# Attention and token/channel mixer on one core: token weights as fp32 over SyncE's queue, first half of c1 in three pieces, more dummies, two opening runs in another order

## The chip, the cores and the metric

One core of one Trainium2 chip runs the kernel. The metric is the time on the device in microseconds (us), the median of three runs: 340.75 us for the kernel before (340.21 to 340.96).

## What is computed

```python
def _attn_ref(q, k, v):                    # 8 batches, 12 heads, 448 tokens, 64 per head
    scores = scale * np.matmul(q, k.transpose(0, 1, 3, 2)) - np.log(S)
    attn = 1.0 / (1.0 + np.exp(-scores))
    return np.matmul(attn, v)

def _moe_ref(x, w_tok1, w_tok2, w_ch1, w_ch2):   # x: 8 x 448 x 768, the heads side by side
    h = np.maximum(x.transpose(0, 2, 1) @ w_tok1, 0.0) @ w_tok2     # 448 -> 256 -> 448
    u = x + h.transpose(0, 2, 1)
    h2 = np.maximum(u @ w_ch1, 0.0) @ w_ch2                         # 768 -> 1536 -> 768
    return u + h2
```

All inputs and the output are fp32; the kernel computes in fp16 with fp32 sums.

## The kernel before

A batch has three units of four heads (two pairs: `g` 0 and 1 on the partitions, `hi` 0 and 1 beside each other), so there are 24 units; the 448 tokens are seven rows `j` of 64. A unit's path is: `q` and `k` are transposed (`tr_q`, `tr_k`), seven score steps `qk(b, u, j)` (L180 to L201: four matmuls of 64x64 into a bank pair of which there are two, then one sigmoid on ScalarE, L194), the value product `av` (L218) into `xa`, copied by VectorE to `xu` (L227), a transpose of `xu` to `xn` (on TensorE with a copy by VectorE in `xtrans`, L252 and L257, or by a transposing DMA from SyncE, L243), the first token product `tok1` (L296, weights `w1`, result in `tk`) with a ReLU to `h`, and the second, `ytrans` (L316, weights `w2`), added to `xu` (L326). When a batch's three units are done, channel products follow: `ch1` (weights `c1`, L364) and `ch2` (weights `c2`, L584). From the second batch on these use seven products in place of eight (`sevens`, L514; L814, L861).

Every engine works its instructions off in the order in which the code lists them (`manual_schedule`); what differs is only how long one waits for another. All loads go through GpSimd's queue (POOL, kind software_dynamic), which also casts fp32 to fp16 under way, and are listed at L945 to L1002: the first `k`, then `q`, `k`, `v` of batch 0 by unit, `w1` (three DMAs, L961 and L965), `w2s` (one, L967), the rest of `v`, batch 1's `q` and `k`, the first half of `c1` (all six 128-row blocks, L976), and so on to `c2` and batch 2. SyncE's queue (SP, kind hardware_dynamic) loads one half of `first_q` at the start; after that its next instruction is the transposing DMA of the second batch's second unit, at 56.30 us, then come the transposes of `q`, `k` and the stores.

The opening (batch 0, L1065 to L1123) is written out by hand: 16 dummy matmuls (`keep_warm`, L1028, on a tile of zeros) stand before the first transposes; then three units of seven scores with other work between them (`between`). `w1` has 448 rows = seven rows `j` of 64, kept as `w1[128, 4, 256]`: rows 2t and 2t+1 in the lower and upper partitions of block t, and row 6 in the lower half of block 3. Its upper half is zeroed at L951 for the first four units and filled with row 6 again by a later DMA (L1189), since `tok_tail` (L277) reads it from both halves. `w2s` is regrouped to `w2` by VectorE (L1051).

The first channel product of batch 0 (`ch1(0, 0, 0, 4)` and two more) takes its blocks in the order 0, 3, 1, 4, 2, 5 (`BY_UNIT`): unit 0's two blocks, unit 1's, unit 2's.

Then two runs written in one loop (L1146 to L1201, `c` 4 and 5: second and third unit of batch 1) weave seven scores, the value product of the unit before and a pair of columns of `ch1` (`ch1_pair`, L387: matmuls of 64x64 in two "turns" of six steps; in the second turn the row halves change places, so each bank gets the other half of the sum). From batch 3 on, `steady(b, u)` (L1305) runs the same plan for each batch; `copies` holds the eight pieces that relayout the next batch's `k` and `q` (L129) and start their transposing DMAs, and `within`, `behind` (L1308) say how many of them are issued at two places of each unit. `gated_loads` (L1125) issues the loads of a later batch after a small copy on GpSimd that waits for the transposed `q`.

Of the kernel before, what the change touches and what calls it, by code (L numbers as in the profile page):

```python
# [9 lines left out]
FP16 = mybir.dt.float16  # L10
# [11 lines left out]
NJ = 7  # L22
NP = 64
NU = 3
# [6 lines left out]
def kernel(  # L31
# [39 lines left out]
    turned = pc.tile([128, 1], FP32, name="turned")  # L71
    w2s = pa.tile([128, 2, S], FP16, tag="parts", bufs=4, name="w2s")
    first_q = pa.tile([128, 2, NJ, E], FP32, tag="parts", bufs=4, name="first_q")
# [14 lines left out]
    def bank(shape, dtype, name):  # L88

        if opening_banks:  # L90
            n = opening_banks.pop(0)
        else:
            n = at_bank[0]
            at_bank[0] = (n + 1) % 4
        return pp.tile(shape, dtype, tag=f"m{n}", bufs=1, name=name)
# [300 lines left out]
    def ch1_pair(b, cb):  # L396

        ps = [bank([128, 512], FP32, f"c1_{b}_{cb + p}") for p in range(2)]

        def step(turn, n):  # L400
            quads(
                ps,
                S,
                turn,
                lambda p, part, m: c1[
                    part, BY_UNIT[n], 128 * (cb + p) + m : 128 * (cb + p) + m + 64
                ],
                lambda p, part: ut(b, BY_UNIT[n])[part, 0:S],
                n == 0,
                n == NDB - 1,  # L410
            )

        def end():
            for p in range(2):
                ch1_out(b, cb + p, ps[p])

        turns = [[lambda t=t, n=n: step(t, n) for n in range(NDB)] for t in range(2)]
        return turns[0], turns[1], end
# [530 lines left out]
    for b in range(2):  # L949
        nc.vector.memset(xu(b)[:, :, :, S:512], 0.0)  # L950
    nc.vector.memset(w1[64:128, 3, :], 0.0)  # L951
    load_first_k(2, NJ)
# [4 lines left out]
    load(0, "k", k, 2, NU)  # L957
    tok_rows = moe_w_tok1.rearrange("(p j) t -> j p t", j=NJ)
    for par in range(2):
        part = slice(64 * par, 64 * par + 64)  # L960
        nc.gpsimd.dma_start(  # L961
            out=w1[part, 0:3, :],
            in_=tok_rows[0:6].rearrange("(t par) p c -> par p t c", par=2)[par],
        )
    nc.gpsimd.dma_start(out=w1[0:64, 3, :], in_=tok_rows[NJ - 1])  # L965
    load(0, "v", v, 1, 2)
    nc.gpsimd.dma_start(  # L967
        out=w2s[:, :, :], in_=moe_w_tok2.rearrange("(tc t) s -> t tc s", tc=2)
    )
    load(0, "v", v, 2, NU)  # L970
    load(1, "q", q, 0, 1)
    load(1, "k", k, 0, 1)

    def load_c1(half):
        cols = slice(CC // 2 * half, CC // 2 * half + CC // 2)
        nc.gpsimd.dma_start(  # L976
            out=c1[:, :, cols],
            in_=moe_w_ch1.rearrange("(db d) c -> d db c", db=NDB)[:, :, cols],
        )

    def load_c2(half):
# [4 lines left out]
        )  # L986

    load(1, "q", q, 1, 2)
    load(1, "k", k, 1, 2)
    load_c1(0)  # L990
    load(1, "v", v, 0, 1)
# [4 lines left out]
    load(2, "q", q, 0, 1)  # L996
    load(2, "k", k, 0, 1)
    load_c2(0)
    load(2, "k", k, 1, NU)
    load(2, "q", q, 1, NU)  # L1000
    load_c2(1)
# [36 lines left out]
    heat[0] = bank([128, 512], FP32, "heat")  # L1038
    keep_warm(16)

# [6 lines left out]
    pe_transpose(0, "k", 0, 0, 2)  # L1047
    keep_warm(3)

    def regroup_w2():  # L1050
# [10 lines left out]
    def tok(u):  # L1061
# [7 lines left out]
            [lambda: keep_warm(4)],  # L1069
            [tp(0, 1, "q")],  # L1070
            [lambda: keep_warm(4)],
# [5 lines left out]
            [value(0, 3, NJ)],  # L1077
            [tp(0, 2, "q")],
            [tp(0, 2, "k")],
# [66 lines left out]
    for c, cb in ((N_FIRST, 3), (N_FIRST + 1, 8)):  # L1146
# [11 lines left out]
        turn0, turn1, end = ch1_pair(0, cb)  # L1158
        if c > N_FIRST:
            qk(b, u, 0)  # L1160
        qk(b, u, 1)
        for f in turn0:
            f()
        qk(b, u, 2)
        av(*before, 0, 4)
        qk(b, u, 3)
        av(*before, 4, NJ)
        if c - 1 in ON_DMA:
            xtrans_dma(*before)
        qk(b, u, 4)  # L1170
        for f in turn1[:4]:
            f()
        qk(b, u, 5)
        for f in turn1[4:]:
            f()
        end()
        qk(b, u, 6)
        if u == 2:
# [7 lines left out]
        if c == N_FIRST:  # L1186
            tok1(*before)
            whole(cb + 4)
            nc.gpsimd.dma_start(out=w1[64:128, 3, :], in_=tok_rows[NJ - 1])  # L1189
            ytrans(*before)  # L1190
        else:
            for w, f in pieces_ch2(0, by_half[:2]):
                f()
                if copies:
                    copies.pop(0)()
            while copies:
                copies.pop(0)()

            nc.gpsimd.tensor_copy(out=gate[:, :], in_=tr[2, "q"][:, 1, NJ - 1, 126:128])
            load(2, "v", v, 1, NU)  # L1200
            gated_loads(b)  # L1201
# [103 lines left out]
    def steady(b, u):  # L1305

        lot, before, ahead = b - 2, divmod(NU * b + u - 1, NU), divmod(NU * b + u - 2, NU)
        within, behind = ((0, 1), (3, 4), (0, 0))[u]  # L1308

# [43 lines left out]
        else:  # L1353
# [5 lines left out]
            run(steps, 5)  # L1359
            send = end(put_off=True)  # L1360
            score()
            at_bank[0] = Y
# [26 lines left out]
        some(behind)  # L1389
        if u == 1 and b < B - 1:  # L1390
            gated_loads(b)
# [102 lines left out]
```

## Time and profile before

| what | value |
|---|---|
| median of three runs | 340.75 us (340.21 to 340.96) |
| profiled execution: time, span from first to last instruction | 341.39 us, 339.6 us |
| first score's sigmoid starts | 8.33 us |
| first matmul on `c1` | 33.70 us |
| two runs of the loop: from, to | 39.3 us, 59 us |
| first `steady` batch: from, to; the next | 102.5 to 140.8 us; 140.8 to 179.1 us |
| first-half `c1` load: issue, landing after | 21.01 us, 12.6 us |
| TensorE's granted clock over the span | 0.998 |

The profiled execution's span is 1.8 us shorter than its time, and its time 0.64 us above the median; times within a trace are counted from the first instruction. In the views of the profile, PE is TensorE's matmuls, PEld its weight loads, DVE VectorE, ACT ScalarE, POOL GpSimd, SP SyncE. A row of the timeline has its start, its length, engine, line, operation, what it writes and reads, how many instructions it merges, and in brackets how long the engine was idle before it and what released it.

### The profile page before, as it was taken

The numbers are of one execution on the slowest core, as the hardware profiler recorded it, in microseconds if no ns is written. First come the engines' busy times: TensorE is split into PE (matmuls) and PEld (weight loads), VectorE is DVE, ScalarE is ACT, GpSimd is POOL, SyncE is SP. The second block draws the span as 40 slices with busy tenths as digits, with TensorE's granted clock in tenths as the row PEclk, the third lists the DMA queues.
The fourth block names the chain that finished last, engine by engine and source line by source line (L and its number), as shares of the span: only waits on it lengthen the run. The fifth ranks groups of instructions, "written<-read, shape, count | busy, mean of one in ns | idle before, by whom it ended". The sixth has DMA issues, their size and how long they took to land.

```text
span 339.6 us, 10285 instructions
## 1 busy us (share of the span) xinstructions
PE 332.2 (98%) x4423; PEld 242.5 (71%) x4423; DVE 234.9 (69%) x484; ACT 213.0 (63%) x272; POOL 58.7 (17%) x102
## 2 busy tenths in 40 slices
PE   7999999999999999999999999999999999999994
PEld 4555565555796679866896679866896679769852
DVE  2277366678998973877768773878758654876882
ACT  3997657388647895578647895578647795314200
POOL 8981550050031000220032002020010000000000
PEclk9999999999999999999999999999999999999999
DMA  7999999999999999998999899988995293028007
GB/s 119 173 174 195 206 205 204 163 175 237 169 187 189 140 168 211 185 142 161 204 145 172 138 206 175 206 117 134 196 175 93 56 193 73 2 56 185 4 11 197
DMA packets 104381, 52.17 MB, mean 154 GB/s; under 512 B 76432, under 2 KB 101264, under 8 KB 104336
## 3 DMA queue, kind: packets, MB, share of 16 engines
q1 hardware_dynamic: 78704, 29.11, 47.8%
q0 software_dynamic: 25168, 21.50, 42.1%
q10 hardware_dynamic: 464, 0.92, 1.0%
q8 instruction: 34, 0.56, 0.7%
q14 instruction: 11, 0.09, 0.1%
HBM read 43.45 MB, written 11.01 MB: 160 GB/s over the span
## 4 chain that ended last, share of the span: by engine, by line
PE 86%; DMA 5%; POOL 4%; ACT 2%; issue 1%; DVE 0%; ACTq 0%; POOLq 0%
PE c_ab L514 14%; PE c L814 10%; PE qk L187 9%; PE c_c L514 8%; PE xa L218 7%; PE c L861 6%; PE tk L296 5%; PE yt L316 5%; PE c L387 4%; DMA c<-in_moe_w_ch_dram 4%; PE c L584 4%; PE c L364 3%; PE c L669 3%; PE c L650 2%; ACT att L194 2%; DMA raw_v<-in_v_dram 2%
## 5 line engine op out<-in xcount | busy, mean ns | idle before, releaser
L194 ACT ACTIVATE att<-qk,att_bias 128x896 f16<-128x896 f32 x168 | 156.0, 1012 | 38.6 <-PE qk L187 37.6
L187 PE MATMUL qk<-tr_q,tr_k 64*64 64x448 f16 x672 | 61.3, 360 | 0.3 <-ACT att L194 0.2
L514 PEld LDWEIGHTS <-c 128*128 128x128 f16 x504 | 48.4, 98 | 1.1 <-issue 0.3
L218 PE MATMUL xa<-att,raw_v 64*64 64x448 f16 x644 | 40.7, 349 | 0.0
L187 PEld LDWEIGHTS <-tr_k 64*64 64x64 f16 x672 | 25.2, 105 | 19.0 <-issue 11.9
L514 PEld LDWEIGHTS <-sum 128*128 128x128 f16 x378 | 36.3, 98 | 0.0
L227 DVE CAST xu<-xa 128x448 f16<-128x448 f32 x40 | 23.1, 619 | 18.8 <-PE xa L218 18.4
L535 ACT ACTIVATE pt_ab<-c_ab 128x896 f32<-128x896 f32 x21 | 19.2, 917 | 20.6 <-PE c_ab L514 20.6
L218 PEld LDWEIGHTS <-raw_v 64*64 64x64 f16 x672 | 22.0, 107 | 8.3 <-issue 0.4
L861 PE MATMUL c<-c,h 64*64 64x384 f16 x360 | 24.6, 322 | 0.0
L1127 POOL COPY gate<-tr_q 128x2 f16<-128x2 f16 x6 | 1.6, 275 | 121.7 <-DMA tr_q<-rel_q 121.7
L326 DVE TENSOR_TENSOR xu<-xu,yt 128x448 f16<-128x448 f16 x38 | 21.7, 613 | 0.0
L537 ACT ACTIVATE h<-c_ab 128x896 f16<-128x896 f32 x7 | 6.4, 917 | 24.4 <-PE c_ab L514 24.4
L296 PE MATMUL tk<-xn,w 128*128 128x256 f16 x156 | 21.2, 274 | 0.1
L544 DVE TENSOR_TENSOR h<-pt_ab,c_ab 128x896 f16<-128x896 f32 x14 | 15.2, 1084 | 8.6 <-PE c_ab L514 8.6
L544 DVE TENSOR_TENSOR h<-pt_c,c_c 128x448 f16<-128x448 f32 x21 | 12.9, 614 | 11.7 <-PE c_c L514 11.6
L316 PE MATMUL yt<-w,h 128*128 128x448 f16 x88 | 20.3, 353 | 0.0
L841 DVE TENSOR_TENSOR o<-un,c 128x384 f32<-128x384 f16 x32 | 17.4, 550 | 4.0 <-PE c L814 4.0
L310 ACT ACTIVATE h<-tk 128x256 f16<-128x256 f32 x42 | 14.2, 406 | 9.5 <-PE tk L296 9.5
L814 PEld LDWEIGHTS <-hid 128*128 128x128 f16 x132 | 12.9, 98 | 8.0
L514 PE MATMUL c_ab<-diffs,c 128*128 128x224 f16 x168 | 18.4, 259 | 0.0
L296 PEld LDWEIGHTS <-w 128*128 128x128 f16 x156 | 13.6, 98 | 5.7 <-issue 2.4
(134 smaller groups left out, 572.1 us busy)
## 6 DMA issues: line engine op xcount, KB each, us to landing
out_dram<-o SPq DMA_DIRECT2D x41, 192.0 KB, 3.2
c<-in_moe_w_ch_dram POOLq DMA_DIRECT2D x4, 1152.0 KB, 16.1
raw_k<-in_k_dram POOLq DMA_DIRECT2D x10, 336.0 KB, 6.9
raw_q<-in_q_dram POOLq DMA_DIRECT2D x10, 336.0 KB, 5.7
raw_v<-in_v_dram POOLq DMA_DIRECT2D x10, 336.0 KB, 8.8
out_dram<-o SPq DMA_DIRECT2D x15, 96.0 KB, 2.4
raw_q<-in_q_dram POOLq DMA_DIRECT2D x12, 112.0 KB, 5.1
raw_k<-in_k_dram POOLq DMA_DIRECT2D x12, 112.0 KB, 5.4
```

Source lines behind the costliest of these rows:

```text
L187: nc.tensor.matmul(out=ps[64 * g : 64 * g + 64, hi, 0:S], lhsT=tr[b, "k"][64 * hi : 64 * hi + 64, u, j, 64 * g : 64 * g + 64], rhs=tr[b, " ...
L194: nc.scalar.activation(out=att[b, u, j][:, :, :], in_=ps[:, :, 0:S], func=SIGMOID, bias=bias_t[:, :], scale=att_scale,)
L218: nc.tensor.matmul(out=ps[g][64 * hi : 64 * hi + 64, 0:S], lhsT=raw[b, "v"][64 * g : 64 * g + 64, u, hi, j, :], rhs=att[b, u, j][64 * g : ...
L227: nc.vector.tensor_copy(out=xu(b)[:, u, g, 0:S], in_=ps[g][:, 0:S])
L296: nc.tensor.matmul(out=ps[tcb], lhsT=w1[rows, t, cols], rhs=xn[b, u][rows, :, t, :], start=(t == 0 and not with_scores), stop=(t == (2 if ...
L316: nc.tensor.matmul(out=ps[:, 0:S], lhsT=h1[b, u][:, tcb, g, :], rhs=w2[:, tcb, :, :], start=(tcb == 0), stop=(tcb == 1),)
L326: nc.vector.tensor_tensor(out=x, in0=x, in1=ps[:, 0:S], op=ADD)
L514: nc.tensor.matmul(out=ps[:, g, p, :], lhsT=weights[n][:, d, 128 * cb : 128 * cb + 128], rhs=moving[n][:, d, :], start=(n in (1, 5, 2) and ...
L535: nc.scalar.activation(out=shaped(part[:, :, :]), in_=ps, func=COPYF)
L544: nc.vector.tensor_tensor(out=shaped(dst), in0=shaped(parts[gs, which]), in1=ps, op=ADD)
L814: nc.tensor.matmul(out=ps[:, 0:DH], lhsT=self.weights[n][:, k, :], rhs=self.moving[n][:, k, :], start=(n in (1, 2, 5) and k == 0), stop=(k ...
L861: nc.tensor.matmul(out=ps[m : m + 64, 0:DH], lhsT=lhsT(n)[part, m : m + 64], rhs=rhs(n)[part, :], start=(opens and turn == 0 and n == 0), ...
```

## The change

- `w1` and `w2s` are loaded as fp32 (`w1s`, `w2s`) by five DMAs on SyncE's queue. They stand behind a memset of one column of `w1s` on VectorE that is listed after the copy of unit 1's `tr_q`. VectorE casts `w1s` to `w1` in one instruction (`cast_w1`), listed between the copies of unit 2's `tr_q` and `tr_k`; both halves of block 3 get row 6, so the zeroing of L951 and the DMA of L1189 go. `regroup_w2` reads fp32.
- The GpSimd queue: without the token weights; `v` of units 1 and 2 in one pair of DMAs; the first half of `c1` by unit (blocks 0 and 3; 1 and 4; 2 and 5), the first piece ahead of batch 1's second unit; batch 2's `k` and `q` of unit 1 ahead of the first half of `c2`.
- 21 dummies in place of 16 at the start.
- In the two runs each score stands one place earlier: `qk` 2 comes after three of the six steps of the first turn, the others follow, and no score is left between the second turn and the plain columns; the third unit's `qk` 0 moves into the first run. `ch1_pair` gets `turn_over`, a copy of one column by VectorE between the turns.
- In batch 3, during which the fifth batch (4) is given its relayouts, the eight pieces are dealt (0, 0), (4, 2), (2, 0) in place of (0, 1), (3, 4), (0, 0), and `gated_loads(3)` comes at the end of unit 2, not 1.

```diff
-    w2s = pa.tile([128, 2, S], FP16, tag="parts", bufs=4, name="w2s")
+    w2s = pa.tile([128, 2, S], FP32, tag="parts", bufs=4, name="w2s")
+    w1s = pa.tile([128, 4, TT], FP32, tag="un", bufs=2, name="w1s")
...
     def ch1_pair(b, cb):
...
+        turn_bank[0] = ps[1]
...
-    nc.vector.memset(w1[64:128, 3, :], 0.0)
...
-    for par in range(2):
-        part = slice(64 * par, 64 * par + 64)
-        nc.gpsimd.dma_start(
-            out=w1[part, 0:3, :],
-            in_=tok_rows[0:6].rearrange("(t par) p c -> par p t c", par=2)[par],
-        )
-    nc.gpsimd.dma_start(out=w1[0:64, 3, :], in_=tok_rows[NJ - 1])
-    load(0, "v", v, 1, 2)
-    nc.gpsimd.dma_start(
-        out=w2s[:, :, :], in_=moe_w_tok2.rearrange("(tc t) s -> t tc s", tc=2)
-    )
-    load(0, "v", v, 2, NU)
+    load(0, "v", v, 1, NU)
...
+    load_c1(0, 0)
     load(1, "q", q, 1, 2)
     load(1, "k", k, 1, 2)
-    load_c1(0)
+    load_c1(0, 1)
+    load_c1(0, 2)
...
+    load(2, "k", k, 1, 2)
+    load(2, "q", q, 1, 2)
     load_c2(0)
-    load(2, "k", k, 1, NU)
-    load(2, "q", q, 1, NU)
+    load(2, "k", k, 2, NU)
+    load(2, "q", q, 2, NU)
...
-    keep_warm(16)
+    keep_warm(21)
...
+    def load_token_weights():
+        rows = moe_w_tok1.rearrange("(p j) t -> j p t", j=NJ)
+        nc.vector.memset(w1s[:, 0, 0:1], 0.0)
+        for par in range(2):
+            part = slice(64 * par, 64 * par + 64)
+            nc.sync.dma_start(
+                out=w1s[part, 0:3, :],
+                in_=rows[0:6].rearrange("(t par) p c -> par p t c", par=2)[par],
+            )
+            nc.sync.dma_start(out=w1s[part, 3, :], in_=rows[NJ - 1])
+        nc.sync.dma_start(
+            out=w2s[:, :, :], in_=moe_w_tok2.rearrange("(tc t) s -> t tc s", tc=2)
+        )
+
+    def cast_w1():
+        nc.vector.tensor_copy(out=w1[:, :, :], in_=w1s[:, :, :])
...
-            [tp(0, 1, "q")],
+            [tp(0, 1, "q"), load_token_weights],
...
-            [tp(0, 2, "q")],
+            [tp(0, 2, "q"), cast_w1],
...
-        if c > N_FIRST:
-            qk(b, u, 0)
         qk(b, u, 1)
-        for f in turn0:
+        for f in turn0[:3]:
             f()
         qk(b, u, 2)
+        for f in turn0[3:]:
+            f()
+        turn_over(turn_bank[0])
+        qk(b, u, 3)
         av(*before, 0, 4)
-        qk(b, u, 3)
+        qk(b, u, 4)
         av(*before, 4, NJ)
...
-        qk(b, u, 4)
+        qk(b, u, 5)
         for f in turn1[:4]:
             f()
-        qk(b, u, 5)
+        qk(b, u, 6)
         for f in turn1[4:]:
             f()
         end()
-        qk(b, u, 6)
...
             tok1(*before)
+            qk(*ahead, 0)
             whole(cb + 4)
-            nc.gpsimd.dma_start(out=w1[64:128, 3, :], in_=tok_rows[NJ - 1])
...
-        within, behind = ((0, 1), (3, 4), (0, 0))[u]
+        within, behind = (
+            ((0, 0), (4, 2), (2, 0)) if b == NU else ((0, 1), (3, 4), (0, 0))
+        )[u]
...
             send = end(put_off=True)
+            some(within)
             score()
...
-        if u == 1 and b < B - 1:
+        if u == (2 if b == NU else 1) and b < B - 1:
             gated_loads(b)
```

More of the change, by code (lines that the diff above doesn't have):

```diff
@@ L410, in step @@
                 n == NDB - 1,
+                True,
             )
@@ L957, with load_c1 @@
     load(0, "k", k, 2, NU)
-    tok_rows = moe_w_tok1.rearrange("(p j) t -> j p t", j=NJ)
-    for par in range(2):
-        part = slice(64 * par, 64 * par + 64)
-        nc.gpsimd.dma_start(
-            out=w1[part, 0:3, :],
-            in_=tok_rows[0:6].rearrange("(t par) p c -> par p t c", par=2)[par],
-        )
-    nc.gpsimd.dma_start(out=w1[0:64, 3, :], in_=tok_rows[NJ - 1])
-    load(0, "v", v, 1, 2)
-    nc.gpsimd.dma_start(
-        out=w2s[:, :, :], in_=moe_w_tok2.rearrange("(tc t) s -> t tc s", tc=2)
-    )
-    load(0, "v", v, 2, NU)
+    load(0, "v", v, 1, NU)
     load(1, "q", q, 0, 1)
     load(1, "k", k, 0, 1)
-    def load_c1(half):
+    def load_c1(half, u=None):
         cols = slice(CC // 2 * half, CC // 2 * half + CC // 2)
+        blocks = slice(0, NDB) if u is None else slice(u, NDB, NU)
         nc.gpsimd.dma_start(
-            out=c1[:, :, cols],
-            in_=moe_w_ch1.rearrange("(db d) c -> d db c", db=NDB)[:, :, cols],
+            out=c1[:, blocks, cols],
+            in_=moe_w_ch1.rearrange("(db d) c -> d db c", db=NDB)[:, blocks, cols],
         )
```

## The prediction

> **What bounds the kernel now.** I read the page first, then the timeline of the opening, that of the two runs, and last what single DMA issues took.
>
> ```profile
> PE 332.2 (98%) x4423; PEld 242.5 (71%) x4423; DVE 234.9 (69%) x484; ACT 213.0 (63%) x272; POOL 58.7 (17%) x102
> ...
> DMA  7999999999999999998999899988995293028007
> ```
>
> TensorE is busy nearly throughout, and the DMA engines (third part of the slices) are full from the second slice to the eighteenth. The two full `steady` batches take 38.3 us each by the stages, with TensorE busy all of it, so little is to be had after 100 us; the change works ahead of that. The opening's timeline:
>
> ```profile
> 1.05 3.59 PE L1028 MATMUL heat<-warm 128*128 128x256 f16 x16 [1.05 <-DVE att_bias L948]
> ...
> 5.83 0.96 PE L170 MATMUL tp_q<-ident,raw_q 128*64 128x128 f16 x14 [1.18 <-DVE raw_q L1041]
> ...
> 7.68 0.96 PE L187 MATMUL qk<-tr_q,tr_k 64*64 64x448 f16 x8
> ...
> 8.33 1.91 ACT L194 ACTIVATE att<-qk,att_bias 128x896 f16<-128x896 f32 x2 [1.01 <-PE qk L187]
> ...
> 10.01 0.55 PE L187 MATMUL qk<-tr_q,tr_k 64*64 64x448 f16 x4
> ...
> 10.61 11.94 ACT L194 ACTIVATE att<-qk,att_bias 128x896 f16<-128x896 f32 x13 [0.38 <-PE qk L187]
> ...
> 11.34 0.58 PE L170 MATMUL tp_q<-ident,raw_q 128*64 128x128 f16 x14
> ...
> 11.96 0.62 DVE L179 COPY tr_q<-tp_q 128x896 f16<-128x896 f16 x1 [2.11 <-PE tp_q L170]
> ...
> 18.04 0.61 DVE L179 COPY tr_k<-tp_k 128x896 f16<-128x896 f16 x1
> ...
> 18.93 0.69 DVE L257 COPY xn<-xb 128x1024 f16<-128x1024 f16 x1 [0.28 <-PE xb L252]
> ...
> 20.07 1.05 PE L296 MATMUL tk<-xn,w 128*128 128x256 f16 x8
> ```
>
> ScalarE sets the pace: from 10.61 its sigmoids follow each other without a gap. TensorE starts slow: 14 transposes take 0.96 us at 5.83 and 0.58 at 11.34, four scores 0.55 at 10.01 and 0.38 later. Ahead of 5.83 TensorE is idle for 1.18 us.
>
> ```profile
> 33.70 0.49 PEld L364 LDWEIGHTS <-c 128*128 128x128 f16 x4 [0.41 <-DMA c<-in_moe_w_ch_dram]
> ...
> 44.42 0.38 PE L187 MATMUL qk<-tr_q,tr_k 64*64 64x448 f16 x4 [0.16 <-ACT att L194]
> 44.43 0.11 PEld L187 LDWEIGHTS <-tr_k 64*64 64x64 f16 x3 [0.58 <-issue]
> ...
> 56.49 0.11 PEld L187 LDWEIGHTS <-tr_k 64*64 64x64 f16 x3 [0.37 <-issue]
> ```
>
> Here TensorE waits: once for `c1`, and in each run for ScalarE before the seventh score (a bank pair is still being read). The last view is the landing time of four issues on SyncE's queue, taken in windows that begin at 56.0, 98.1, 98.7 and 133.5 us:
>
> ```profile
> xn<-xu SPq DMA_TRANSPOSE x1, 10.1
> ```
> ```profile
> out_dram<-o SPq DMA_DIRECT2D x1, 96.0 KB, 5.2
> ```
> ```profile
> out_dram<-o SPq DMA_DIRECT2D x1, 96.0 KB, 6.6
> ```
> ```profile
> out_dram<-o SPq DMA_DIRECT2D x1, 96.0 KB, 2.3
> ```
>
> The same store lands in 2.3 us with GpSimd's queue empty and in 5.2 and 6.6 us with 336 KB loads of that queue under way; a transposing DMA took 10.1 us while `c2` was loading.
>
> **The start.** Sixteen dummies take 3.59 us, so 21 take 3.59 x 21/16 = 4.7 and end at 5.76, just ahead of the transposes at 5.83: nothing is delayed. What it buys is the fast pace sooner. TensorE came to it between 9.65 (last slow dummies) and 10.48, some 4.2 us after 5.83; 4.2 us after 1.05 would be 5.3. Then the 14 transposes save 0.38, the four of `k` 0.43 - 0.58 x 4/14 = 0.26, the three dummies 0.82 - 0.50 = 0.32: 0.96 at most for the first sigmoid, nothing if the pace comes after 7.7. To this comes that the 0.38 gap of ScalarE before its third sigmoid closes, as the work in it (ten transposes, three dummies) shrinks as well. That is 1.34 if the pace comes by 5.8 and 0.4 if it comes after 7.7. VectorE's and ScalarE's copies on this path (0.43, 0.49) do not shrink, so I take 1.0. The Trainium skill (TensorE: Matmul & The Clock Gate, section Part 1: The HAM clock gate) has the clock judged over free-running windows of about 3.4 us, of which one must be busy. By that the pace would come anywhere from 4.5 to 7.9 us; at the late end 0.4 of the start would be left and the sum below would be -0.8 in place of -1.4. That the trace's pace came near 10 us, between one and two such windows after 5.83, agrees with it.
>
> **The token weights.** GpSimd loses five issues of 0.5 to 0.74 us, and SyncE gets five in a stretch where nobody is queued behind them until 56.30. They wait for a memset behind `tr_q`'s copy, which ended at 12.59 and would end at 11.6. At 0.65 us an issue (rows of 0.5 to 0.77 on that queue) the fourth, the last of `w1`, is issued at 13.55. Its landing is the open term. Bounds: 2.3 us (empty queue) and 10.1. The loads of GpSimd's queue ahead of it here are 112 and 224 KB, not 336: the 2.9 us that the first store lost scales to 1.9. So 13.55 + 2.3 + 1.9 = 17.8. VectorE is ready for the cast at 18.04 - 1.0 = 17.1 and is held for 0.7. Behind the cast stand `tr_k`'s copy (unit 2's scores wait for it) and `xn` (the first token product waits). The cast is priced by the `xn` row, 1024 elements in 0.69 (at most twice the 0.43 of the 512-element cast at 5.35, 0.86). Then 17.8 + 0.1 + 0.69 + 0.61 + 0.69 less two overlaps of 0.08 = 19.75, where TensorE would be ready at 19.07. ScalarE has no slack there, as its gap before the next sigmoid is 0.04, so all of it counts: against 20.07 the opening gains 0.3 of the 1.0. Each microsecond of landing is a microsecond of the result.
>
> `regroup_w2` reads fp32 in place of fp16: 0.88 now; between 0.88 and twice that. It is followed by a product that waits for it (0.35 in the trace); I take +0.05, as rows per element of fp32 casts are no slower than copies, +0.9 at the far end. Its load is issued 0.65 later than `w1`'s last and needed 3 us later, which covers it. The memset and `turn_over` (0.15 each, rows of L852) fall into idle time of VectorE (1.88 us before the value copy at 42.62); without that cover each costs 0.15.
>
> **c1 in pieces.** The last weight load before it ends at 33.29 (0.41 ahead), and others follow within 0.1, so 0.3 is lost to `c1`. Of its 1152 KB, 5.7 us at the 206 GB/s of that stage, the first two thirds now suffice to go on, which is 1.9 us sooner, and the token weights have left the queue. Batch 1's second `q` and `k` move behind the first piece: they landed at 23.7 and 25.9 and are read at 31.5. Gain 0.3, range 0 to 0.4. Two more issues of 0.84 on GpSimd are covered, as it sits idle for 6.74 us at 27 to 34.
>
> **The two runs.** Place by place, with four scores 0.19 us of TensorE, 24 quarter matmuls 1.17, sixteen of the value product 0.75 and twelve 0.56: the first run's plain columns start 5.41 us after its first score (39.33 to 44.74), by the sum without a wait 4.9. In the new order the scores are 0.75 to 0.94 apart, at or above the 0.89 of a sigmoid, so the wait goes: 0.5. The second run loses 0.11 and 0.29 to the same: 0.4. I take 0.85; if the waits only move, 0.
>
> **Batch 2 and the fifth batch.** `k` and `q` of unit 1 come ahead of `c2`'s half, which landed at 53.56, is read at 60.09 and comes some 2 us later: covered, by 4 us. In batch 3 the pieces move on VectorE, 0.53 each, but SyncE's transposes of `k` and `q` are issued at 117.5 and 128.85, behind a store and the 5 us transposing issue of `un`; `q`'s last relayout would end near 122. `gated_loads` waits for the same landing (134.59). Nothing moves: 0, -0.1 to +0.5 (the stage is TensorE's).
>
> **Sum.** -0.3 (opening) + 0.05 - 0.3 - 0.85 = -1.4 against the span of 339.6, or 341.39 - 1.4 = 340.0 for the profiled execution. That execution is 0.64 above the median, so from 340.75: 339.3.
>
> **Rivals.** (1) The token weights land in time, by 17.0. Then the start's whole 1.0 is kept: -1.0 - 0.3 - 0.85 = -2.15: 338.6. For it: the loads are small, and the queue is not deep at 12 us (loads land 4.7 us after issue, of which 2 to 3 are their own). Against it: four of them in a row. The Trainium skill (DMA: Bandwidth & Descriptors, section Queues, rings and completion order) says that an engine takes turns between queues after 9 to 17 descriptors. By that rule the loads would have a turn every microsecond, which is this rival; the 10.1 us of the transpose disagree.
>
> (2) Slower: SyncE's loads are served only after the backlog of GpSimd's queue, as the transpose at 56.30 was. Place: the cast on VectorE. It turns the sum positive when the fourth load takes over 5.6 us (17.8 + 1.4 = 19.2). At the 6.6 of the second store, landing at 20.15, it is +1.0: 341.7; at 10.1 it is +4.4: 345.2. For it: two of the three loaded rows are above 5.6. Against it: these had 336 KB or `c2` loads ahead.
>
> (3) The gains don't add: the runs' waits only move to the next place, or the earlier work meets DMAs that don't come earlier (the transpose of 56.30 lands at 66.36 and is read at 68.4; the next at 74.76, read at 76.34, 1.6 us of room). Then -0.3 - 0.3 = -0.6 and 340.1, no change that can be told.
>
> **Chances.** Forecast 0.42, (1) 0.28, (2) 0.13, (3) 0.17. The forecast's own range is 338.8 to 340.0. The range of 8 in 10 runs from 338.2 (rival 1 with 1.3 at the start) to 341.6 (rival 2 at its mildest). A change of 0.2% (0.7 us, 340.07 and 341.43) is about what can be told from none here: faster takes the forecast but for 0.02, (1), and a quarter of (3), 0.72; slower (2) but for 0.02, 0.11; the rest is the same.
>
> **What would show it.** Right: transposes of 0.6 us at 5.8 and a third sigmoid near 9.6; a cast that waits for `w1s` some 0.7 us; the token product near 19.7; no wait for `c1`; no wait for ScalarE at the seventh score. Wrong: a wait of 2 us or more on the cast, with ScalarE idle behind it; `turned` holding TensorE; a `steady` batch other than 38.3.

## The result: 346.33 us in place of 340.86

The changed kernel takes 346.33 us (median of 5 runs, 345.31 to 346.43), the kernel before in the same series 340.86 (340.21 to 341.01); the ratio is 1.0156, with a 95% interval of 1.0138 to 1.0173. Ratios below are against the kernel before on the same chip, and leave out runs that lie over 1.5% above the fastest of their kernel; medians and ranges are of all runs of a kernel.

The profiled execution has a span of 344.1 us and a time of 345.84. From the page of the profile after, first part, second part (the granted clock) and fourth part (the chain that ended last, by line):

```profile
PE 333.7 (97%) x4428; PEld 243.6 (71%) x4428; DVE 235.8 (69%) x487; ACT 212.7 (62%) x272; POOL 58.1 (17%) x101
...
PEclk9989999999999999999999999999999999999999
...
PE c_ab L517 14%; PE qk L188 10%; PE c L817 10%; PE xa L219 9%; PE c_c L517 8%; PE c L864 6%; PE tk L297 6%; PE c L388 5%; PE yt L317 5%; PE c L587 3%; PE c L672 3%; PE c L365 3%; PE c L653 2%; DMA w1s<-in_moe_w_tok_dram 2%; DMA first_q<-in_q_dram 1%; PE c L894 1%
```

TensorE works 1.5 us longer than before on nearly the same instructions, the granted clock dips in the third slice, and the load of `w1s` has come onto the chain with 2% of the span, some 7 us. The timeline of the opening after (start, length, engine, line, operation; in brackets the idle time before and what ended it):

```profile
6.37 0.86 PE L171 MATMUL tp_q<-ident,raw_q 128*64 128x128 f16 x14 [0.65 <-DVE raw_q L1036]
...
8.24 12.68 ACT L195 ACTIVATE att<-qk,att_bias 128x896 f16<-128x896 f32 x14 [0.48 <-PE qk L188]
...
11.74 0.06 DVE L1047 MEMSET w1s<- 128x1 f32 x1
...
21.82 0.69 DVE L1060 CAST w<-w1s 128x1024 f16<-128x1024 f32 x1 [4.27 <-DMA w1s<-in_moe_w_tok_dram]
22.42 0.62 DVE L180 COPY tr_k<-tp_k 128x896 f16<-128x896 f16 x1
...
22.96 0.68 DVE L258 COPY xn<-xb 128x1024 f16<-128x1024 f16 x1
```

The same, from the answer for 18 to 28 us:

```profile
23.69 1.55 PE L297 MATMUL tk<-xn,w 128*128 128x256 f16 x8 [4.14 <-DVE xn L258]
25.18 0.59 PE L188 MATMUL qk<-tr_q,tr_k 64*64 64x448 f16 x4
25.88 1.01 ACT L195 ACTIVATE att<-qk,att_bias 128x896 f16<-128x896 f32 x1 [4.96 <-PE qk L188]
...
27.73 1.01 ACT L195 ACTIVATE att<-qk,att_bias 128x896 f16<-128x896 f32 x1 [0.85 <-PE qk L188]
```

The cast waits 4.27 us for `w1s`. The copies of `tr_k` and `xn` queue behind it on VectorE, TensorE stands still for 4.14 us ahead of the token product, and ScalarE for 4.96 us. When TensorE goes on, it is slow: four scores take 0.59 us in place of 0.38, and ScalarE waits another 0.85 us before the next sigmoid. Busy times and granted clock by stretch (the column after POOL is the clock):

```profile
20.00:24.00 4.00, 0.31 (x3) 0.38 (x4) 1.82 (x3) 0.92 (x2) 2.39 (x4) 1.00 1.15 250
24.00:28.00 4.00, 4.00 (x43) 2.01 (x45) 1.66 (x3) 1.28 (x2) 2.76 (x4) 0.57 1.20 207
```

Before, the stretch from 24 to 28 us had a clock of 1.00 and 68 matmuls, not 43:

```profile
24.00:28.00 4.00, 4.00 (x68) 2.56 (x72) 3.20 (x7) 3.97 (x5) 2.64 (x5) 1.00 1.06 174
```

The transfers: in the kernel before, the three loads of `w1` on GpSimd's queue, issued from 10.08 to 11.60, had all landed by 15.42. The time from issue to landing, from the answer for 10 to 17 us:

```profile
w<-in_moe_w_tok_dram POOLq DMA_DIRECT2D x2, 96.0 KB, 4.4
w<-in_moe_w_tok_dram POOLq DMA_DIRECT2D x1, 32.0 KB, 3.8
```

After, from the answers for single stretches: the time from issue to landing of `w1s`'s first and fourth load (issued 11.82 and 13.86, landed 18.86 and 21.69), then the queues from 12.0 to 15.7 us, and from 15.8 to 20.9 us (q0 is GpSimd's, q1 SyncE's). A queue's row has its packets, its MB, and the time of its packets as a share of that of the 16 engines; packets that overlap bring it above 100%.

```profile
w1s<-in_moe_w_tok_dram SPq DMA_DIRECT2D x1, 192.0 KB, 7.0
```
```profile
w1s<-in_moe_w_tok_dram SPq DMA_DIRECT2D x1, 64.0 KB, 7.8
```
```profile
q0 software_dynamic: 775, 0.64, 116.6%
q8 instruction: 1, 0.02, 1.6%
```
```profile
q0 software_dynamic: 703, 0.62, 73.8%
q1 hardware_dynamic: 643, 0.65, 44.6%
```

SyncE's queue moves nothing for the first 4 us after its issue; then it gets about every second packet, beside the last loads of batch 0 and those of batch 1, which stood behind the token weights in the order before.

Where the time went, by the start of the same sigmoid in both traces (after less before), in us:

| place | offset | step |
|---|---|---|
| third to 14th sigmoid (ahead of the token product) | -0.60 | -0.60 |
| first token product (TensorE) | +3.62 | +4.22 |
| 16th sigmoid, then steady to `c1`'s first product | +5.24 | +1.62 |
| behind `c1`'s first product | +4.93 | -0.30 |
| behind the two runs | +4.69 | -0.24 |
| batches 3 and 5, then steady to the last | +4.88 | +0.19 |

The span grew by 4.5, not 4.9: from the issue of the last store to the end of the span it is 0.4 us less than before (3.4 in place of 3.9).

### The profile page after: what moved, and what is told of

Its sections match the earlier page's. It is cut to its first block, busy times and chain, and to the rows that moved or that the text cites. A ratio compares the mean times of both kernels' runs of the same rounds, so it can differ in the third digit from the quotient of the medians.

```text
span 344.1 us, 10307 instructions
## 1 busy us (share of the span) xinstructions
PE 333.7 (97%) x4428; PEld 243.6 (71%) x4428; DVE 235.8 (69%) x487; ACT 212.7 (62%) x272; POOL 58.1 (17%) x101
## 4 chain that ended last, share of the span: by engine, by line
PE 92%; DMA 4%; DVE 2%; SPq 1%; issue 0%; ACT 0%; DVEq 0%; ACTq 0%
PE c_ab L517 14%; PE qk L188 10%; PE c L817 10%; PE xa L219 9%; PE c_c L517 8%; PE c L864 6%; PE tk L297 6%; PE c L388 5%; PE yt L317 5%; PE c L587 3%; PE c L672 3%; PE c L365 3%; PE c L653 2%; DMA w1s<-in_moe_w_tok_dram 2%; DMA first_q<-in_q_dram 1%; PE c L894 1%
## 5 line engine op out<-in xcount | busy, mean ns | idle before, releaser
L219 PE MATMUL xa<-att,raw_v 64*64 64x448 f16 x644 | 41.7, 355 | 0.0
L228 DVE CAST xu<-xa 128x448 f16<-128x448 f32 x40 | 23.1, 620 | 17.9 <-PE xa L219 17.5
L538 ACT ACTIVATE pt_ab<-c_ab 128x896 f32<-128x896 f32 x21 | 19.2, 917 | 20.6 <-PE c_ab L517 20.6
L297 PEld LDWEIGHTS <-w 128*128 128x128 f16 x156 | 13.8, 99 | 10.0 <-issue 3.7
L844 DVE TENSOR_TENSOR o<-un,c 128x384 f32<-128x384 f16 x32 | 17.5, 552 | 4.1 <-PE c L817 4.1
```

The source lines that it names most:

```text
L219: nc.tensor.matmul(out=ps[g][64 * hi : 64 * hi + 64, 0:S], lhsT=raw[b, "v"][64 * g : 64 * g + 64, u, hi, j, :], rhs=att[b, u, j][64 * g : ...
L228: nc.vector.tensor_copy(out=xu(b)[:, u, g, 0:S], in_=ps[g][:, 0:S])
L297: nc.tensor.matmul(out=ps[tcb], lhsT=w1[rows, t, cols], rhs=xn[b, u][rows, :, t, :], start=(t == 0 and not with_scores), stop=(t == (2 if ...
L538: nc.scalar.activation(out=shaped(part[:, :, :]), in_=ps, func=COPYF)
```

## The experiments

The first four kernels ask which part is the loss, and by what.

**weights_back.** The token weights as before the change, all else as after.

```diff
-    load(0, "v", v, 1, NU)
...
+    nc.gpsimd.dma_start(out=w1[0:64, 3, :], in_=tok_rows[NJ - 1])
+    load(0, "v", v, 1, 2)
+    nc.gpsimd.dma_start(
...
-            [tp(0, 1, "q"), load_token_weights],
+            [tp(0, 1, "q")],
...
-            [tp(0, 2, "q"), cast_w1],
+            [tp(0, 2, "q")],
```

> The changed kernel with w1 and w2s in fp16 over GpSimd's queue again, as before the change; the rest of the change stays. Theory 'late load': all of the loss comes from the token weights' landing, and what is left are the gains read from the changed kernel's trace by place: opening -0.60 (sigmoids 3 to 13), c1 -0.30, the two runs -0.24, batches 3 and 4 +0.19, in all -0.95: 339.9 us against 340.86, no wait of VectorE for weights, token product at 19.4 to 19.5. Rival 'the rest costs too' (other order of GpSimd's loads, more dummies): the time stays above 341.5.

341.44 us (11 runs, 340.15 to 346.65), ratio 1.0021 (1.0004 to 1.0038). The loss is gone, but no gain is left either. The trace shows both: the offset is -1.43 through the opening, -1.71 behind `c1`, -1.54 at 84 us, and +1.12 at 103 us. The theory holds for the weights (the token product starts at 18.66); its time of 339.9 missed a loss of 2.7 us near 87 us, taken up below.

**weights_alone.** The kernel before, with the token weights' part alone.

```diff
+    w1s = pa.tile([128, 4, TT], FP32, tag="un", bufs=2, name="w1s")
...
-            [tp(0, 1, "q")],
+            [tp(0, 1, "q"), load_token_weights],
...
-            [tp(0, 2, "q")],
+            [tp(0, 2, "q"), cast_w1],
```

> The kernel before with the token weights alone over SyncE's queue in fp32 and the cast. Theory 'late load': the gate comes 0.85 us later than in the changed kernel (no shorter start), the fourth load lands some 7.8 us after its issue, so near 22.6, the token product starts near 24.5 in place of 20.07, and the slow clock behind it adds 1.6: 340.86 + 4.4 + 1.6 = 346.9. Rival 'the pieces of c1 ahead of batch 1 make the load late': without them the fourth load takes some 5 us, lands at 19.7, and the time is 342.5 or less.

348.02 us (4 runs, 346.91 to 353.56), ratio 1.0208 (1.0185 to 1.0230). The fourth load, issued at 14.53, landed at 22.54 (8.0 us), and the token product started at 24.54. The pieces of `c1` are not what makes the load late; this one edit makes the whole loss. It makes 1.1 us more of it than forecast: TensorE stood for 4.63 us, the granted clock behind that was low from 23.5 to 30.3 us, not for 3.4 us as in the kernel after, and the offset settled at +7.19.

**dummies_in_wait.** The kernel after, with 24 more dummies ahead of the token product.

```diff
-            [tok(0)],
+            [lambda: keep_warm(24), tok(0)],
```

> The changed kernel with 24 dummies more ahead of the first token product, in the time in which TensorE waits (19.6 to 23.6). Theory 'clock': the wait of over 3.4 us takes TensorE's fast pace away, which costs 1.6 us behind it (from +3.62 at the token product to +5.24 at the second sigmoid after it); with the dummies, 344.7 in place of 346.3, and a token product of 1.05 us in place of 1.94. Rival 'only the wait counts': 346.3, as ScalarE is the pace behind it anyway.

345.02 us (4 runs, 343.76 to 351.18), ratio 1.0118 (1.0094 to 1.0143): 1.3 less than after. Its timeline and, below it, its stretch from 24 to 28 us:

```profile
19.04 2.79 PE L1023 MATMUL heat<-warm 128*128 128x256 f16 x24
23.53 1.03 PE L297 MATMUL tk<-xn,w 128*128 128x256 f16 x8 [1.69 <-DVE xn L258]
```
```profile
24.00:28.00 4.00, 4.00 (x66) 2.08 (x65) 3.23 (x6) 2.98 (x4) 2.88 (x4) 1.00 1.20 208
```

The token product starts as late as in the kernel after (0.16 sooner), but takes 1.03 us, the clock stays at 1.00, and the offset behind it is +3.44 in place of +5.24. From the token product to the next sigmoids nothing is lost here, so the 1.62 us in the table is the clock, lost by standing still.

**weights_early.** The kernel after, with the gate and the five loads ahead of the first unit's scores.

```diff
+    load_token_weights()
...
-            [tp(0, 1, "q"), load_token_weights],
+            [tp(0, 1, "q")],
```

> The changed kernel with the gate and the five loads ahead of the first unit's scores, so issued from about 7.7 us, not 11.8. Theory 'the delay is the queue's depth at the issue': the fourth load, issued at 9.8, lands 6 to 7.8 us later, at 16 to 17.6, the cast at 17.5 does not wait, the token product starts at 19.6 to 19.9, and the time is 339.6 to 340.2. Rival 'the engines' time is what is short': the loads take their share from batch 0's q, k and v, the third unit's k lands 1.5 to 3 us later than at 15.9, scores wait for it, and the time is 341.5 to 343.5.

13 runs from 340.30 to 351.31, median 343.93, ratio 1.0035 (1.0007 to 1.0063). The runs lie in two groups: six from 340.30 to 341.23, as fast as the kernel before, and seven from 343.93 up. The one profile is of the slowest run, and shows the rival at its place: the fourth load, issued at 8.83, landed at 17.29 (8.5 us), so that the cast waited 0.61 us only, but the third unit's `k` landed at 17.5 and 19.2 in place of 13.8 and 15.9 in the kernel after, and TensorE waited:

```profile
PE tp_k L171 <- DMA raw_k<-in_k_dram: 2.8, 1, 2.8
```

In this run the queue was no faster at the earlier issue, and what the weights gain is taken from loads that are needed sooner. The same profile lost another 7.3 us near 80 us to a late `xn`. The six runs near 341 are too fast to have lost as much there, and no profile shows what went otherwise in them: whether the earlier issue takes the loss away in about half of the executions stays open.

Then: is it the queue, the type, or the company?

**fp32_on_pool.** The kernel after with the same fp32 loads and the same cast, issued by GpSimd at the old place.

```diff
-    load(0, "v", v, 1, NU)
...
+        nc.gpsimd.dma_start(
+            out=w1s[part, 0:3, :],
...
+        nc.gpsimd.dma_start(out=w1s[part, 3, :], in_=w1_rows[NJ - 1])
...
-            [tp(0, 1, "q"), load_token_weights],
+            [tp(0, 1, "q")],
```

> The changed kernel with w1s and w2s in fp32 and the cast, but loaded over GpSimd's queue at the place where the fp16 weights stood (five DMAs, the two of row 6 among them). Theory 'the other queue is the loss, not the type': the engines' time is nearly the same (512 packets of 1024 B at 57 ns against 448 of 512 B at 60 ns), the weights land by 18, the cast waits under 0.7 us, the token product starts at 19.4 to 20.1, and the time is 340.5 to 342.0. Rival 'fp32 and the cast are the loss': the cast still waits for 2 us or more, or holds the token product past 21, and the time is above 343.

```profile
16.63 0.84 DVE L1058 CAST w<-w1s 128x1024 f16<-128x1024 f32 x1
...
18.64 0.61 PE L297 MATMUL tk<-xn,w 128*128 128x256 f16 x4
```

The four loads, issued from 10.13 to 12.33, landed by 16.55. The cast waits for nothing, and the token product starts at 18.64, 1.43 ahead of the kernel before and 5.05 ahead of the kernel after. At its place the theory is right: up to the token product the type and the cast cost nothing, the other queue does. Behind it 0.46 us went near 24 us, where batch 1's `q` landed at 23.23, not at 21.14 as in weights_back; whether the wider loads made it late was not tried. The time misses the theory, 343.58 us (5 runs, 340.80 to 344.55; ratio 1.0056, 1.0018 to 1.0094): the offset was -1.52 at 65 us, -0.72 at 71 us and +1.96 at 104 us, the loss near 87 us again, with another ahead of it.

**others_wait.** The kernel after, in which GpSimd issues batch 1's loads and what is behind them only when `w1s` has landed.

```diff
+    def later_loads():
+        nc.gpsimd.tensor_copy(out=gate[:, :], in_=w1s[:, 3, TT - 2 : TT])
+        load(1, "q", q, 0, 1)
...
```

> The changed kernel in which GpSimd issues batch 1's loads and all behind them only when w1s has landed (a copy of its last elements on GpSimd stands ahead of them). Theory 'two queues share the engines': SyncE's loads still wait for what GpSimd's queue holds at 11.8 (first packet near 15.8), but then have the engines alone: the fourth lands at 17.8 to 18.7 in place of 21.69, the token product starts at 19.9 to 20.6, TensorE keeps its fast pace, and the time is 341 to 342.5. Rival 'SyncE's queue is slow of itself': the fourth load lands at 20.5 or later all the same, and the time is 344 or more.

345.57 us (4 runs, 344.54 to 347.05), ratio 1.0136 (1.0095 to 1.0178). Neither is right: the fourth load landed between the two forecasts. Of the time, 3.0 us were lost near 90 us (offset +2.60 at 86 us, +5.65 at 103). The timeline, and the queues from 13.8 to 16 us and from 16 to 19 us:

```profile
10.97 0.61 SPq L1053 DMA_DIRECT2D w1s<-in_moe_w_tok_dram  x1
11.62 2.03 SPq L1057 DMA_DIRECT2D w1s<-in_moe_w_tok_dram  x1
13.70 0.60 SPq L1053 DMA_DIRECT2D w1s<-in_moe_w_tok_dram  x1
...
19.88 0.69 DVE L1064 CAST w<-w1s 128x1024 f16<-128x1024 f32 x1 [3.19 <-DMA w1s<-in_moe_w_tok_dram]
```
```profile
q0 software_dynamic: 355, 0.30, 85.3%
q1 hardware_dynamic: 229, 0.22, 32.6%
```
```profile
q1 hardware_dynamic: 558, 0.67, 82.9%
q0 software_dynamic: 95, 0.08, 15.8%
```

The first packet came 2.7 us after the issue, the queues still shared until 16 us (loads of batch 0), and then SyncE's had the engines nearly alone; but one of its issues took 2.03 us in place of 0.6, so the fourth load was issued at 14.34 and landed at 19.76. That is 5.4 us after its issue, in place of 7.8: the loads behind the weights cost 2.4 us of it. From the first issue to the fourth landing it is 8.8 us in place of 9.9, although the four issues took 1.3 longer. What is left is the start of the queue, batch 0's loads, and SyncE's own issue. How these three divide was not tried.

Why is the rest of the change, 1.5 us ahead at 71 us in weights_back, not faster?

**old_loads, dummies_alone, runs_alone.** weights_back with the old order of GpSimd's queue; the kernel before with 21 dummies; the kernel before with the runs' new order.

```diff
-    load_c1(0, 0)
     load(1, "q", q, 1, 2)
     load(1, "k", k, 1, 2)
-    load_c1(0, 1)
-    load_c1(0, 2)
+    load_c1(0)
...
```
```diff
-    keep_warm(16)
+    keep_warm(21)
```
```diff
         qk(b, u, 1)
-        for f in turn0:
+        for f in turn0[:3]:
             f()
         qk(b, u, 2)
...
```

> The kernel with the token weights back on GpSimd's queue and now also the old order of that queue: c1's first half in one load, batch 2's k and q of unit 1 behind c2's half. What is left of the change are the dummies, the runs' order and batch 3's pieces. Theory 'the loads set the pace until 85 us': work that comes earlier meets the same landings (transposes of xn behind batch 3's k and q near 75 us), so most of the 1.0 to 1.4 of the start is lost again and the time is 340.0 to 341.5, as with the new order of loads (341.4). Rival 'the new order of the loads is what cost': with the old one the gains stay and the time is 339.0 to 339.8.

> The kernel before with 21 dummies in place of 16, nothing else. Theory 'start': the fast pace comes ahead of the first scores, the third sigmoid starts 0.6 to 1.4 earlier (9.2 to 10.0), and this offset is still there at c1's first product unless c1 is late by it; at the end 340.0 to 341.0, as c1 lands when it landed (33.6) and takes most of it back. Rival 'all of it comes through': 339.5 to 339.9.

> The kernel before with the two runs' new order alone. Theory from the changed kernel's trace: place by place the runs gain 0.19 and 0.47 and lose 0.42 between them, 0.24 in all: offset -0.2 to -0.3 at the end of the second run, and 340.3 to 340.9 in time. Rival (the prediction's term): -0.85 at that place and 340.0 in time.

341.26 (12 runs, 339.92 to 342.29), 341.00 (10 runs, 340.03 to 341.98) and 340.73 us (10 runs, of which 345.31 and one far out are not in the ratio), with ratios of 1.0011 (0.9993 to 1.0030), 1.0010 (0.9991 to 1.0029) and 1.0005 (0.9984 to 1.0025): none differs from before. What the traces show is in their places. In runs_alone, with 16 dummies, the opening happened to be 1.43 ahead all the same, and `c1`, undivided, took 1.0 of it back; the runs then gained 0.24. In old_loads, 1.73 ahead, `c1` took back 1.1. TensorE's waits from 20 to 40 us, in old_loads and then in runs_alone:

```profile
PE c L364 <- DMA c<-in_moe_w_ch_dram: 1.2, 1, 1.2
```
```profile
PE c L364 <- DMA c<-in_moe_w_ch_dram: 1.1, 1, 1.1
```

In weights_back, with `c1` in pieces, there is no such wait. So the pieces do work where the opening is early: 1.4 ahead, runs_alone lost 1.0 at that place and weights_back gained 0.3. In the kernel after they are not shown to be worth anything: weights_alone, whose `c1` is undivided, has the same -0.30 there (+7.19 to +6.88), since its opening is late. Where `c1` lands differs by execution too: in dummies_alone, 0.99 ahead, it landed undivided at 32.73, 0.9 sooner than before, and took back 0.06. dummies_alone kept its -0.93 until 114 us, and lost 1.4 there.

**q3_later, both_later, before_both_later.** The loss near 87 us begins with the transposing DMA of `xn` issued near 75 us, while GpSimd's four 336 KB loads of batch 3's `k` and `q` are under way. These kernels issue `q` only when that transpose has landed; the second and third also hold batch 4's `k` in the same way.

```diff
-        with_q = b < 2
+        with_q = False
...
         xtrans_dma(*before)
+        if c == 2 * NU + 1:
+            nc.gpsimd.tensor_copy(out=gate[:, :], in_=xn[before][:, 0, 0, 126:128])
+            load(3, "q", q, 0, NU)
```

> The kernel with the token weights back on GpSimd's queue, and batch 3's q loaded only when the transposing DMA of xn issued near 74.7 us has landed. Theory 'transposes lose to loads of 336 KB under way': with two such loads in place of four ahead of it that transpose takes 3 to 6 us, not 12.6, TensorE does not wait for it, the offset of -1.5 at 71 us is still there at 103 us, and the time is 339.0 to 340.2. Rival 'the loads only come later': raw_q lands after 87, its relayout is late, and the time is 341.4 or more.

> As the run before, and batch 4's k also issued only after the transposing DMA near 106 us has landed. Theory 'transposes lose to loads': both places are free, no wait for xn by TensorE over 0.3 us between 70 and 120 us, a time of 338.9 to 339.9 and runs that lie closer together than those of the kernel before (1 us or less between fast runs). Rival 'other transposes wait in their place' (c2's load near 55 to 66, or k of batch 4 too late near 122): 340.7 or more.

> The kernel before with these two later loads and nothing else. Theory 'the kernel before is also held there in some executions': its fast runs, 339.5 to 342.3 now, come together at the lower end, 339.5 to 340.5. Rival 'only the changed phase collides': same as before, median 340.7 to 341.2.

349.95 (6 runs, 343.76 to 352.58), 351.35 (6 runs, 347.57 to 353.70) and 351.86 us (4 runs, 351.38 to 352.12); the last two have ratios of 1.0265 (1.0225 to 1.0306) and 1.0312 (1.0289 to 1.0336). For q3_later, of which one run took 343.76 and five 349.21 or more, there is no ratio. The rivals of the first two hold; for before_both_later neither forecast does. From the timeline of q3_later:

```profile
94.67 0.62 DVE L129 COPY rel_q<-raw_q 128x896 f16<-128x896 f16 x1 [10.24 <-DMA raw_q<-in_q_dram]
```

`raw_q` landed at 94.64, and VectorE, with the channel products' sums queued behind that copy, stood for 10.24 us; in both_later the same wait is 8.3 us. In before_both_later the larger loss, 8.3 us of the offset, comes near 120 us, where VectorE waited 5.8 us ahead of the relayout of batch 4's `k`. Yet the same kernels show the collision. Issue to landing of that one transpose, in the kernel before, in weights_back, in weights_back_2 and in before_both_later, where GpSimd's queue had run dry:

```profile
xn<-xu SPq DMA_TRANSPOSE x1, 6.9
```
```profile
xn<-xu SPq DMA_TRANSPOSE x1, 12.6
```
```profile
xn<-xu SPq DMA_TRANSPOSE x1, 11.0
```
```profile
xn<-xu SPq DMA_TRANSPOSE x1, 3.0
```

Twelve profiles have this transpose with the four loads as they were. Its time goes with how far behind the last of their issues it is issued: 11.0 to 13.0 us at 0.4 to 1.1 us behind, 6.9 to 10.1 at 2.3 to 2.7 (2.7 in the kernel before), 4.8 to 5.0 at 4.3 to 5.7 (4.3 in the kernel after), and 6.0 at 7.2 in weights_early, where another transpose was still under way. GpSimd issued that last load at 73.59 us before and at 73.63 in weights_back, so a kernel that is ahead meets the loads closer.

**xn_on_pe, before_xn_on_pe, weights_back_2.** weights_back with that one transpose on TensorE; the same on the kernel before; and weights_back again.

```diff
-        xtrans_dma(*before)
+        if c != 2 * NU + 1:
+            xtrans_dma(*before)
...
         spent += work(1)
+        if c == 2 * NU + 1:
+            at_bank[0] = 0
+            xtrans(*before)
```

> The kernel with the token weights back on GpSimd's queue, and the xn whose transposing DMA is issued near 74.7 us transposed on TensorE and copied by VectorE instead, behind the channel products that follow. Theory 'what the rest of the change gains ahead of 71 us is lost to that transposing DMA, which GpSimd's loads of batch 3 delay and which delays them': the wait for xn (0.9) and for raw_q behind it (2.7 on VectorE) go, the eight transposes cost TensorE 0.6, so the offset at 103 us is -1.5 + 0.6 to -1.5 + 1.0 and the time 339.8 to 340.6, with its median below that of the same kernel without this edit. Rival 'any order loses there, the loads are the pace': raw_q lands at 86 or later all the same and the time is 341.2 or more.

> The same edit on the kernel before, as a control. By the first theory it costs the 0.6 of the transposes where its transposing DMA landed in time (83.17, read at 87.9): 341.3 to 341.7. If that DMA holds the kernel before in most executions, it gains: below 340.7.

> The kernel with the token weights back on GpSimd's queue once more, on the same chip as these two, for the comparison: 340.5 to 342.0 by the first series; a profile in which xn issued near 74.7 lands by 84 should show an offset of -1.3 to -1.5 at 103 us and 340.4 or less (theory), and about the same time as the late one if the landing does not matter (rival).

341.97 us (12 runs, 341.32 to 346.80), ratio 1.0030 (1.0005 to 1.0054); 342.78 (5 runs, 341.69 to 343.25), 1.0037 (1.0016 to 1.0057); 341.62 (12 runs, 339.98 to 343.91), 1.0008 (0.9984 to 1.0033). In xn_on_pe nothing is lost between 80 and 103 us any more (offset -0.14 throughout), but the edit itself took 1.74 (-1.88 to -0.14), not the 0.6 forecast: 0.7 for the transposes, and a wait of 1.0:

```profile
PE tk L277 <- DVE xn L257: 1.0, 1, 1.0
```

The token product behind it waits until VectorE has copied `xn` away. The control shows the same (-0.55 to +1.18), so beside the edit itself xn_on_pe lost nothing there, where weights_back lost 2.7. weights_back_2 gives a second profile: its transpose landed at 85.43, not 87.35, TensorE did not wait for `xn`, and the offset went from -1.83 to -0.81 at 102 us (a wait for VectorE of 0.9), in place of -1.54 to +1.12; the two profiled executions of one kernel took 340.85 and 342.45. So the loss near 87 us differs by execution. Why the loads and the transpose share the engines better in one execution than in another of the same kernel stays open, and no version that ran is faster than the kernel before.

A smaller loss stands ahead of that one, at the transposing DMA issued near 55 us. It landed at 66.54 in weights_back, 67.62 in fp32_on_pool and 67.23 in q3_later, about when it landed before (66.36), where it was read at 68.4. The token product of a kernel that is 1.5 to 2.0 us ahead waits for it, and 0.42, 0.80 and 1.45 us of the lead went there.

## Why the prediction was wrong, step by step

**The step that failed** is the landing of the token weights: "The loads of GpSimd's queue ahead of it here are 112 and 224 KB, not 336: the 2.9 us that the first store lost scales to 1.9. So 13.55 + 2.3 + 1.9 = 17.8." The issue was nearly right (13.86). The 4.2 us after it were 7.8. The scaling counted only loads that stand ahead; the runs showed a start of 2.4 to 4.0 us in which the queue moves nothing, and then a share of about half with everything that GpSimd issues afterwards. The rows at hand (5.2, 6.6 and 10.1 us under way) had bounded it rightly; choosing a value below all three was the error. Rival 2 was the case that came, with its breakeven of 5.6 us. The Trainium skill's rule of turns between queues (DMA: Bandwidth & Descriptors, section Queues, rings and completion order) fits what the trace shows once the queue has started, 643 packets of one and 703 of the other; it did not make the loads timely, as rival 1 took from it.

**What hangs on it was right.** From 17.8 to 21.69 is 3.9, and each microsecond was to be one of the result: 19.75 + 3.9 = 23.65 for the token product, measured 23.69, and 339.3 + 3.9 = 343.2 for the time.

**A term was missing**: the clock behind a stall. Rival 2 counted the wait alone. Standing still for 4.14 us cost another 1.62, which dummies_in_wait takes away. The granted clock was 0.51 from 24.1 to 27.5 us. The Trainium skill (TensorE: Matmul & The Clock Gate, section Part 1: The HAM clock gate), which has the clock halved after an idle window of about 3.4 us, was weighed for the start, and not for this stall.

**The two runs**: forecast -0.85, measured -0.24, in the kernel after and in runs_alone. The first run shrank from 5.41 to 5.22 us and the second by 0.47, but the score that moved between them added 0.42 there, where it was counted as free. The wait for ScalarE at the seventh score is gone, as forecast, but the first run's sum of 4.9 is not reached: ScalarE's sigmoids came 0.95, 0.95 and 1.08 us apart there, not 0.89. What holds that run is not shown. The premise was wrong in itself: scores 0.75 to 0.94 apart are not all at or above 0.89. The term was mis-sized, as rival 3 has it in part.

**The start**: forecast -1.0, taken from one profile of before. Measured -0.60 in the profile after, whose `first_q` landed 0.4 later (5.63 against 5.25). The mechanism was right (the third sigmoid is 1.7 to 1.8 us behind the first in place of 2.28), but the reference was a draw: the fast pace that came at 10.5 us there came at 5.8 in another profile with 16 dummies (last section).

**c1**: forecast -0.3, measured -0.30, by luck: the late opening gives the same with `c1` undivided (weights_alone). **regroup_w2**: 0.98 in place of 0.88 us, off the path. **The fifth batch**: forecast 0 within -0.1 to +0.5, measured +0.07 in batch 3 and nothing in batch 4, which keeps its 38.3 us. Another +0.12 came at 187 us, in batch 5; weights_back, which has the same edit, does not show it.

Summed: 343.2 + 1.62 (clock) + 0.61 (runs) + 0.19 (batches 3 and 5) = 345.6, beside 346.33 measured and 345.84 for the profiled execution. By the profiles alone the same terms give -1.4 + 3.9 + 1.62 + 0.61 + 0.19 = 4.9, and the offset is 4.88. And even with the weights in time, 338.6 (rival 1) would not have come: weights_back took 341.44 and 341.62. The range's lower half rested on gains that meet the same transfers between 66 and 87 us. Rival 3, 340.1, had this mechanism, and named the transposes that land at 66.36 and 74.76; the first cost up to 1.45, and the greater loss came at the third, issued near 75 us.

## What to carry to other kernels

A second DMA queue is no second set of engines: where the engines are full, moving a load to another queue gives up its place in the order, and it then lands behind or beside everything that the first queue has issued; take its landing from the worst row of such a transfer, not from a scaled best one. Put what can be late at the end of an in-order engine's list, or count every instruction behind it, and add the slow clock that follows when TensorE stands still: in these profiles it came with each of eight waits of 2.7 to 5.6 us, for 3.4 or 6.8 us, and with none of 2.2 us or less behind the opening. And compare a gain at the start with several profiles of the kernel before, since one of them is a draw.

## What the runs showed of the hardware

The fast pace at the start is a matter of phase. Sixteen dummies, from 1.06 to 4.66 us, were followed by transposes at full pace in runs_alone and at the slow one in the kernel before; and 21 dummies by slow transposes in dummies_alone. The dummies and transposes of runs_alone, and the transposes of dummies_alone:

```profile
1.06 3.60 PE L1030 MATMUL heat<-warm 128*128 128x256 f16 x16 [1.06 <-DVE att_bias L950]
...
5.79 0.58 PE L170 MATMUL tp_q<-ident,raw_q 128*64 128x128 f16 x14 [1.14 <-DVE raw_q L1043]
```
```profile
5.83 0.96 PE L170 MATMUL tp_q<-ident,raw_q 128*64 128x128 f16 x14
```

The first dummy or transpose at full pace started between 4.0 and 7.3 us in twelve profiles with 21 dummies, and at 3.8, 5.8, 9.2, 10.3 and 10.5 us in five with 16. The one that came at 3.8 fell back to a granted clock of 0.5 from 7.2 to 10.6 us, behind a wait of 1.78 us. In these profiles, then, five more dummies take the late cases away. That agrees with the free-running windows which the Trainium skill describes (TensorE: Matmul & The Clock Gate, section Part 1: The HAM clock gate). Its idle window of about 3.4 us is longer than what was needed here: the clock fell with waits of 2.83 us (weights_early) and 3.05 us (others_wait) too.

A packet's time hardly differed by the type: 512 packets of 1024 B on SyncE's queue took 57 ns each, 448 of 512 B (fp16) on GpSimd's queue 60 ns. One transposing DMA of `xn` took 3.0 us with GpSimd's queue dry and 4.8 to 13.0 us beside its four 336 KB loads, the longer the closer behind them, and these loads landed up to 4.6 us later as well (`raw_q` at 87.12 in weights_back, 82.49 before, from issues 0.04 us apart).
